# Expert operands as scaled fp16 pairs, and the last 64 slots of each expert in both column halves

## The chip, the cores and the metric

The kernel runs on one core of a Trainium2 chip. The metric is device time in microseconds for one execution; a program is timed in several runs, and their median counts. The engines are named as in the profile: PE is TensorE (matmuls), PEld its weight loads, DVE VectorE, ACT ScalarE, POOL GpSimd, SP SyncE, which here issues most of the DMA transfers. GpSimd issues the indirect ones (gathers and scatters by a list of row numbers).

## The reference, cut to what matters

An attention with a recurrent state (4 batches, 8 heads, 768 steps, head size 40) gives 3072 rows of 320 features. These rows go through a mixture of 8 experts, of which each row takes two:

```python
logits = x @ w_gate
noisy_logits = logits + np.log1p(np.exp(x @ w_noise)) * noise
top2 = np.argpartition(-noisy_logits, 2, axis=1)[:, :2]
...
for e in range(E):                       # E = 8
    for k in range(2):
        mask = top2[:, k] == e
        h = np.maximum(x[mask] @ w1[e], 0.0)          # 320 -> 1024
        out[mask] += top2_w[mask, k, None] * (h @ w2[e])   # 1024 -> 320
```

All inputs and the output are fp32.

## The kernel before, in words

**Stages.** The attention runs first, in 24 chunked steps. Each finished block of 128 rows is written to DRAM (`xd`) and gets its expert logits; after some blocks at a time `route` ranks the rows within their expert, and GpSimd scatters an entry for each row (row number, weight) into a list of slots per expert in DRAM (`ls`). `flag` then computes a word `fi`, which says whether the fast path was allowed. After that come the experts. At the end of the program every engine loads `fi` and branches: if it is set, a second pass with slots that overflowed (`extra`) runs, and behind it a general version of the whole.

**An expert** has 832 slots, in two parts of 512 and 320 (`PARTS`), or six tiles of 128 slots and one of 64. For each expert:

- SP loads the weights (`load1` into `w1r`, `load2` into `w2r`) and the slot list (`loadx` into `le`, which has two buffers; `w1r`, `w2r` and `xr` have one). GpSimd gathers the 832 rows into `xr`, one indirect transfer for each tile.
- `split1`, `split2`: each weight becomes a pair, its rounding (`w1h`, `w2h`, written by ScalarE) and the rest (`w1l`, `w2l`, written by VectorE).
- `trans`: TensorE transposes the rows into `pt`, and ScalarE and VectorE write them as pairs (`xh`, `xl`, and `x3`, `x3l` for the last 64 features).
- `hidden`: for each of 8 groups of 128 hidden features, 8 matmuls into one `ph` buffer (of three): high times high, low times high and high times low. ScalarE writes the relu as `hh`, VectorE the rest as `hl`.
- `output`: for each tile of slots, 24 matmuls of 320 columns into one `po` buffer (of three), ScalarE scales by the routing weight into `y`, and GpSimd adds `y` to the output rows by an indirect transfer that accumulates.

Both operands of these matmuls are `fp32r` tiles before. Of the tile with 64 slots the loaded operand is 64 columns wide: half of the array's columns stand unused.

**Order.** The code writes expert e's `hidden` and `output` with the loads, splits and transposes of expert e + 1 between them. The order on each engine is set by the tile framework's scheduler (`schedule_with_timeline_sim=True`), which simulates the program with its own costs. Each engine, and each queue of transfers that it issues, then works through its list in that order and waits where a semaphore says so. The first expert's part 0 has a priority, so that it starts while the last routing round runs. Its second part and all later experts read the list after the last scatter.

Of the kernel before, what the change touches and what calls it, by code (L numbers as in the profile page):

```python
# [41 lines left out]
class Moe:  # L42
# [180 lines left out]
    def split2(s,w):
        nc=s.nc
        h=s.wp.tile([128,8,DM],F32R,name="w2h"); l=s.wp.tile([128,8,DM],F32R,name="w2l")
        for k in range(0,8,2):
            nc.scalar.activation(h[:,k:k+2],w[:,k:k+2],AF.Copy)
            nc.vector.tensor_tensor(l[:,k:k+2],w[:,k:k+2],h[:,k:k+2].bitcast(F32),op=ALU.subtract)
        return h,l
    def loadx(s,e,X=None,part=0):  # L230
# [12 lines left out]
        return X
    def trans(s,x,X=None,part=0):

        nc=s.nc
# [4 lines left out]
        t0,n=s.parts[part]; t0%=CAP
        for k in range(3):
# [4 lines left out]
            if k<2:  # L257
                nc.scalar.activation(xh[:,k,r],pt[:,:n],AF.Copy)  # L258
                nc.vector.tensor_tensor(xl[:,k,r],pt[:,:n],xh[:,k,r].bitcast(F32),op=ALU.subtract)
            else:  # L260
                for q in (slice(0,64),slice(64,128)): nc.scalar.activation(x3[q,r],pt[64:128,:n],AF.Copy)
                for q in (slice(0,64),slice(64,128)): nc.vector.tensor_tensor(x3l[q,r],pt[64:128,:n],x3[64:128,r].bitcast(F32),op=ALU.subtract)
        return X
    def hidden(s,W,X,part):
        nc=s.nc; wh,wl=W; xh,xl,x3,x3l=X
        t0,n=s.parts[part]; t0%=CAP; r=slice(t0,t0+n)
        hh=s.hp.tile([128,8,n],F32R,name=f"hh{part}"); hl=s.hp.tile([128,8,n],F32R,name=f"hl{part}")
        for f in range(8):
# [605 lines left out]
```

## Time and profile before

| what | us |
|---|---|
| median of 3 runs | 1047.81 |
| the runs | 1039.84, 1050.55, 1047.81 |
| span of the profiled execution | 1041.6 |
| TensorE busy in it | 786.2 |
| VectorE, ScalarE, GpSimd busy | 498.1, 396.3, 473.4 |
| experts, about | 606 to 1030 |

The span is the time from the first to the last instruction that the profiler saw on the core. The profiled execution has no time of its own beside its span; the median of the runs stands 6.2 us above it. Times in the rows below count from the start of the span.

### The profile page before, as it was taken

What the parts mean: (1) busy time and instruction counts of PE and PEld (TensorE: products, weight loads), DVE (VectorE), ACT (ScalarE), POOL (GpSimd) and SP (SyncE); (2) the same over time, 40 slices, a digit from 0 to 9 for tenths busy, and PEclk for the clock granted to TensorE, in tenths of its full rate; (3) what the DMA queues carried; (4) which work ended last, traced back from release to release, by engine and by line L of the source; (5) the groups of instructions that cost most, each with busy time, mean ns of one, the idle gap of its engine ahead of it and who ended that gap; (6) DMA issues with size and microseconds to landing.
All of it is one profiled execution on the core that took longest, in us unless ns stands there. A gap on an engine that the chain in (4) does not pass through costs nothing.

```text
span 1041.6 us, 25165 instructions
## 1 busy us (share of the span) xinstructions
PE 786.2 (75%) x10570; PEld 696.0 (67%) x10570; DVE 498.1 (48%) x951; ACT 396.3 (38%) x816; POOL 473.4 (45%) x616
## 2 busy tenths in 40 slices
PE   0111043968767687998869469999999999999995
PEld 0111043757656575887658349999999999999995
DVE  9369924464566454456345442534343334433420
ACT  2213322444443353564434322534343434343421
POOL 6202478056786848818830324133333333333313
PEclk9999996789897886999969579999999999999998
DMA  3789863487488558665335743425252525252303
GB/s 100 184 199 254 237 175 79 114 220 203 121 205 235 101 128 216 161 149 146 89 82 157 228 151 62 132 49 136 59 135 60 140 56 137 57 139 57 36 7 38
DMA packets 135263, 136.20 MB, mean 131 GB/s; under 512 B 67392, under 2 KB 114948, under 8 KB 135060
## 3 DMA queue, kind: packets, MB, share of 16 engines
q1 hardware_dynamic: 123492, 117.35, 42.9%
q0 software_dynamic: 11648, 17.15, 9.3%
q8 instruction: 85, 1.39, 0.6%
q14 instruction: 38, 0.31, 0.1%
HBM read 96.48 MB, written 41.37 MB: 132 GB/s over the span
## 4 chain that ended last, share of the span: by engine, by line
PE 48%; POOL 18%; DMA 15%; DVE 7%; issue 5%; SPq 4%; ACT 2%; POOLq 0%; ACTq 0%; DVEq 0%
PE po L286 19%; PE ph L273 17%; POOL X L534 6%; POOL Tt L533 5%; POOL ls L161 3%; DMA rawk<-in_fm_dram 3%; PE pt L255 2%; DMA d_ab<-pk 2%; PE pY L433 2%; PE pW L433 2%; PE psc L433 2%; DMA xr<-xd,le 2%; DMA le<-ls 1%; DMA raww<-in_fm_dram 1%; DVE pk L423 1%
## 5 line engine op out<-in xcount | busy, mean ns | idle before, releaser
L289 POOL DMA_INDIRECT out_dram<-y,le x56 | 93.6, 1672 | 204.4 <-ACT y L288 202.3
L275 DVE SCALAR_TENSOR_TENSOR hl<-ph,hh 128x320 fp32r<-128x320 f32 (+1 forms) x128 | 75.4, 591 | 156.9 <-ACT hh L274 156.7
L274 ACT ACTIVATE hh<-ph 128x320 fp32r<-128x320 f32 (+1 forms) x128 | 66.1, 518 | 153.5 <-PE ph L273 153.4
L242 POOL DMA_INDIRECT xr<-xd,le x56 | 54.0, 964 | 92.0 <-DMA le<-ls 44.6
L534 POOL TENSOR_TENSOR X<-X,Tt 128x30 f32<-128x30 f32 (+9 forms) x150 | 85.2, 568 | 10.5
L286 PE MATMUL po<-w2h,hh 128*128 128x320 f32 (+1 forms) x448 | 87.2, 314 | 0.0
L533 POOL TENSOR_TENSOR Tt<-X 128x30 f32<-128x30 f32 (+9 forms) x150 | 81.6, 544 | 10.0
L286 PE MATMUL po<-w2l,hh 128*128 128x320 f32 (+1 forms) x448 | 78.2, 312 | 0.0
L286 PE MATMUL po<-w2h,hl 128*128 128x320 f32 (+1 forms) x448 | 77.6, 309 | 0.0
L286 PEld LDWEIGHTS po<-w2h,hh 128*128 128x128 f32 (+1 forms) x448 | 70.7, 180 | 4.2
L273 PE MATMUL ph<-xh,w1h 128*128 128x512 f32 (+1 forms) x256 | 71.3, 362 | 0.5 <-ACT xh L258 0.5
L273 PE MATMUL ph<-xh,w1l 128*128 128x512 f32 (+1 forms) x256 | 69.4, 352 | 0.0
L273 PE MATMUL ph<-xl,w1h 128*128 128x512 f32 (+1 forms) x256 | 69.0, 351 | 0.0
L433 PE MATMUL pQ<-w,dT 128*128 128x40 f16 x1152 | 41.6, 186 | 35.3 <-DMA d_k<-pk 27.2
L286 PEld LDWEIGHTS po<-w2h,hl 128*128 128x128 f32 (+1 forms) x448 | 67.6, 180 | 0.8
L286 PEld LDWEIGHTS po<-w2l,hh 128*128 128x128 f32 (+1 forms) x448 | 67.2, 180 | 1.2
L433 PEld LDWEIGHTS <-dT 128*128 128x128 f16 x1152 | 39.0, 101 | 42.8 <-DMA d_k<-pk 27.5
L433 PEld LDWEIGHTS <-st_ab 120*64 120x64 f16 (+1 forms) x928 | 26.6, 117 | 60.6 <-issue 26.6
L433 PE MATMUL psc<-RV,uT 128*64 128x128 f32 x384 | 59.8, 306 | 7.3 <-DVE P L657 6.8
L433 PE MATMUL psc<-RV 128*64 128x128 f32 x384 | 59.9, 306 | 0.0
L288 ACT ACTIVATE y<-po,le 128x320 f32<-128x320 f32 (+1 forms) x56 | 29.5, 526 | 79.1 <-PE po L286 79.1
L657 DVE TENSOR_TENSOR P<-psc,mk 128x512 f32<-128x512 f32 x48 | 33.0, 687 | 54.7 <-PE psc L433 54.6
(282 smaller groups left out, 1857.3 us busy)
## 6 DMA issues: line engine op xcount, KB each, us to landing
w2r<-in_w_dram SPq DMA_DIRECT2D x8, 1280.0 KB
RV<-in_rv_dram SPq DMA_DIRECT2D x48, 192.0 KB
rawba<-in_fm_dram SPq DMA_DIRECT2D x24, 360.0 KB
d_ab<-pk SPq DMA_DIRECT2D x24, 360.0 KB
st_ab<-d_ab SPq DMA_DIRECT2D x36, 240.0 KB
w1r<-in_w_dram SPq DMA_DIRECT2D x8, 1024.0 KB
raww<-in_fm_dram SPq DMA_DIRECT2D x12, 365.6 KB
st_ab<-d_ab SPq DMA_DIRECT2D x24, 180.0 KB
```

The lines of the kernel that those rows point to most:

```text
L161: st=nc.gpsimd.indirect_dma_start(out=s.ls[s.half],out_offset=OFFS(ap=po[:,j,k:k+1],axis=0),in_=s.ent[:,j,k],in_offset=None)
L242: for k in range(c,c+a): nc.gpsimd.indirect_dma_start(out=x[:p,k],out_offset=None,in_=s.xd[w],in_offset=OFFS(ap=li[:p,k,0:1],axis=0))
L273: for i,(a,b) in enumerate(mm): nc.tensor.matmul(ph[:,:n],a,b,start=i==0,stop=i==7)
L274: nc.scalar.activation(hh[:,f],ph[:,:n],AF.Relu)
L275: nc.vector.scalar_tensor_tensor(hl[:,f],ph[:,:n],0.0,hh[:,f].bitcast(F32),op0=ALU.max,op1=ALU.subtract)
L286: nc.tensor.matmul(po[:p],h[:,f,r],w[:,f],start=k==0,stop=k==23); k+=1
L288: nc.scalar.activation(y[:p],po[:p],AF.Copy,scale=w_[:p,ii:ii+1])
L289: st=nc.gpsimd.indirect_dma_start(out=s.out_d,out_offset=OFFS(ap=idx[:p,ii],axis=0),in_=y[:p],in_offset=None,compute_op=ALU.add)
L433: def mm(s,*a,**k): return lambda: s.nc.tensor.matmul(*a,**k)
L533: eng.tensor_tensor(t,Xt[:,j:j+1,j+1:].to_broadcast([128,j,m]),Xt[:,0:j,j:j+1].to_broadcast([128,j,m]),op=ALU.mult)
L534: s.tl=eng.tensor_tensor(Xt[:,0:j,j+1:],Xt[:,0:j,j+1:],t,op=ALU.add)
L657: nc.vector.tensor_tensor(m,pp.rearrange("p i j t->p (i j) t"),s.mk.to_broadcast([128,8,64]),op=ALU.mult)
```

## The change

The tiles of the expert operands become `F16`. So that high and low part lie in the range of fp16, the operands are scaled while they are split: rows by `XE` = 2^8, `w1` by `WE` = 2^6, `w2` by `VE` = 2^6; ScalarE's copy takes the scale, and VectorE's subtraction becomes one fused multiply and subtract. The routing weights take the inverse, `YS`, in `route`.

fp16 has less range, so guards are added, each a VectorE reduction into a column of its own. `sized` takes the maximum of a piece of each weight (256 or 320 elements in each partition) and of a tile of rows, which is compared with `LEAST` at the end. `finite` adds up `w1l` (2048 elements), the lower half of `w1h` (1024) and each `y` (320, or 160 in the last tile), and the sum is tested for being a number. `verdict` puts all of them together after the last expert, in nine VectorE instructions and one matmul, and writes `fi`. So `fi`, which was ready ahead of the experts, is ready only behind them.

In `output` the tile of 64 slots (c = 2) now has 48 matmuls of 160 columns: the 64 slots stand in the lower column half of the array with the first 160 output features and in the upper half with the others. Its `y` has 128 rows of 160 features, and the scatter writes half rows by the index `ix2` = 2 × row + half. For this the slot list of that tile is loaded into both halves of the partitions, with a fourth load of `le`.

```diff
+XE,WE,VE=2.0**8,2.0**6,2.0**6
+YS=1/(XE*WE*VE)
+LEAST=2.0**-9
...
         oh=s.gate(lg,s.nz[:,n0:n0+T],T,w[:,:,0],w[:,:,1])
+        nc.vector.tensor_scalar(w,w,YS,None,op0=ALU.mult)
...
+    def sized(s,a):
+
+        if s.nm<2*E_+1: s.nc.vector.tensor_reduce(s.mx[:,s.nm:s.nm+1],a,axis=AX.X,op=ALU.max); s.nm+=1
+    def finite(s,a,q=0):
+
+        s.nc.vector.tensor_reduce(s.yc[q:128,s.ny:s.ny+1],a,axis=AX.X,op=ALU.add); s.ny+=1
...
     def split1(s,w):
         nc=s.nc
-        h=s.wp.tile([128,3,FF],F32R,name="w1h"); l=s.wp.tile([128,2,FF],F32R,name="w1l")
+        h=s.wp.tile([128,3,FF],F16,name="w1h"); l=s.wp.tile([128,2,FF],F16,name="w1l")
         for k in (0,1,2):
-            nc.scalar.activation(h[:,k],w[:,k],AF.Copy)
-            if k<2: nc.vector.tensor_tensor(l[:,k],w[:,k],h[:,k].bitcast(F32),op=ALU.subtract)
-            else: nc.vector.tensor_tensor(h[64:128,k],w[64:128,k],h[64:128,k].bitcast(F32),op=ALU.subtract)
+            nc.scalar.activation(h[:,k],w[:,k],AF.Copy,scale=WE)
+            if k<2: nc.vector.scalar_tensor_tensor(l[:,k],w[:,k],WE,h[:,k],op0=ALU.mult,op1=ALU.subtract)
+            else: nc.vector.scalar_tensor_tensor(h[64:128,k],w[64:128,k],WE,h[64:128,k],op0=ALU.mult,op1=ALU.subtract)
+        s.sized(w[:,0,0:256])
+        s.finite(l.rearrange("p k f->p (k f)")); s.finite(h[64:128,2],64)
         return h,l
     def split2(s,w):
         nc=s.nc
-        h=s.wp.tile([128,8,DM],F32R,name="w2h"); l=s.wp.tile([128,8,DM],F32R,name="w2l")
+        h=s.wp.tile([128,8,DM],F16,name="w2h"); l=s.wp.tile([128,8,DM],F16,name="w2l")
         for k in range(0,8,2):
-            nc.scalar.activation(h[:,k:k+2],w[:,k:k+2],AF.Copy)
-            nc.vector.tensor_tensor(l[:,k:k+2],w[:,k:k+2],h[:,k:k+2].bitcast(F32),op=ALU.subtract)
+            nc.scalar.activation(h[:,k:k+2],w[:,k:k+2],AF.Copy,scale=VE)
+            nc.vector.scalar_tensor_tensor(l[:,k:k+2],w[:,k:k+2],VE,h[:,k:k+2],op0=ALU.mult,op1=ALU.subtract)
+        s.sized(w[:,0])
...
             nc.sync.dma_start(l[:p,c:c+a],s.ls[w][b:b+a*p].rearrange("(p a) f->p a f",p=p))
+            if p==64: nc.sync.dma_start(l[64:128,c:c+a],s.ls[w][b:b+a*p].rearrange("(p a) f->p a f",p=p))
...
-                nc.scalar.activation(xh[:,k,r],pt[:,:n],AF.Copy)
-                nc.vector.tensor_tensor(xl[:,k,r],pt[:,:n],xh[:,k,r].bitcast(F32),op=ALU.subtract)
+                nc.scalar.activation(xh[:,k,r],pt[:,:n],AF.Copy,scale=XE)
+                nc.vector.scalar_tensor_tensor(xl[:,k,r],pt[:,:n],XE,xh[:,k,r],op0=ALU.mult,op1=ALU.subtract)
...
-        hh=s.hp.tile([128,8,n],F32R,name=f"hh{part}"); hl=s.hp.tile([128,8,n],F32R,name=f"hl{part}")
+        hh=s.hp.tile([128,8,n],F16,name=f"hh{part}"); hl=s.hp.tile([128,8,n],F16,name=f"hl{part}")
...
+            c=128//p; d=DM//c
             k=0
             for h,w in ((hh,wh),(hl,wh),(hh,wl)):
                 for f in range(8):
-                    nc.tensor.matmul(po[:p],h[:,f,r],w[:,f],start=k==0,stop=k==23); k+=1
+                    for j in range(c): nc.tensor.matmul(po[p*j:p*j+p,:d],h[:,f,r],w[:,f,d*j:d*j+d],start=k==0,stop=k==23)
+                    k+=1
             y=s.yp.tile([128,DM],F32,name="y",bufs=8)
-            nc.scalar.activation(y[:p],po[:p],AF.Copy,scale=w_[:p,ii:ii+1])
-            st=nc.gpsimd.indirect_dma_start(out=s.out_d,out_offset=OFFS(ap=idx[:p,ii],axis=0),in_=y[:p],in_offset=None,compute_op=ALU.add)
+            nc.scalar.activation(y[:,:d],po[:,:d],AF.Copy,scale=w_[:,ii:ii+1])
+            s.finite(y[:,:d])
+            if c==1: o_,ix,yv=s.out_d,idx[:,ii],y
+            else:
+                ix=s.yp.tile([128,1],I32,name="ix2"); nc.vector.scalar_tensor_tensor(ix,idx[:,ii],2.0,s.half2,op0=ALU.mult,op1=ALU.add)
+                o_=s.out_d.rearrange("n (j d)->(n j) d",j=2); yv=y[:,:d]
+            st=nc.gpsimd.indirect_dma_start(out=o_,out_offset=OFFS(ap=ix,axis=0),in_=yv,in_offset=None,compute_op=ALU.add)
...
+        s.ny=s.nm=0
+        s.yc=t("yc",[128,E_*(NTT+5)]); nc.gpsimd.memset(s.yc,0.0)
+        s.mx=t("mx",[128,2*E_+1])
+        s.half2=t("half2",[128,1]); nc.gpsimd.memset(s.half2,0.0); nc.gpsimd.memset(s.half2[64:128],1.0)
+    def verdict(s):
+
+        nc=s.nc; t=lambda n,sh,dt=F32: s.kp.tile(sh,dt,name=n)
+        z=t("vz",[128,E_*(NTT+5)]); nc.vector.tensor_tensor(z,s.yc,s.yc,op=ALU.subtract)
+        nc.vector.tensor_scalar(z,z,0.0,None,op0=ALU.is_equal)
+        v=t("vv",[128,2*E_+2]); nc.vector.tensor_reduce(v[:,0:1],z,axis=AX.X,op=ALU.min)
+        nc.vector.tensor_scalar(v[:,1:],s.mx,LEAST,None,op0=ALU.is_ge)
+        vh=t("vh",[128,2*E_+2],F16); nc.vector.tensor_copy(vh,v)
+        pv=s.pt.tile([128,2*E_+2],F32,name="pt",bufs=2); nc.tensor.matmul(pv,s.ones,vh,start=True,stop=True)
+        b=t("vb",[128,2*E_+2])
+        nc.vector.tensor_scalar(b,pv,0.5,None,op0=ALU.is_lt)
+        nc.vector.tensor_scalar(b[:,0:1],pv[:,0:1],127.5,None,op0=ALU.is_lt)
+        w=t("vw",[128,1]); nc.vector.tensor_reduce(w,b,axis=AX.X,op=ALU.max)
+        g=t("vg",[128,2]); nc.vector.tensor_tensor(g,s.ff,w.to_broadcast([128,2]),op=ALU.max)
+        nc.vector.tensor_copy(s.fl,g)
...
             x=s.loadx(0); W1=s.split1(r1); X=s.trans(x[0])
+            s.sized(x[0][:,0])
...
             if e+1<E_: W2=s.split2(r2); x=xn
+        s.verdict()
```

`x3`, `x3l`, `hl` and the other tiles change in the same way.

**Order on SyncE**, in the middle of the experts: the issues of the loads for one expert (`w1r`, `w2r` weights, `le` slot list) and the first for the one after. Before:

```order
L208 DMA w1r<-in_w_dram 128x2x1024
L209 DMA w1r<-in_w_dram 64x1024 x2
L213 DMA w2r<-in_w_dram 128x8x320
L241 DMA le<-ls_843 128x16
L241 DMA le<-ls_843 128x8
L241 DMA le<-ls_843 64x4
L208 DMA w1r<-in_w_dram 128x2x1024
```

Now:

```order
L218 DMA w1r<-in_w_dram 128x2x1024
L219 DMA w1r<-in_w_dram 64x1024 x2
L254 DMA le<-ls_843 128x16
L254 DMA le<-ls_843 128x8
L254 DMA le<-ls_843 64x4
L255 DMA le<-ls_843 64x4
L223 DMA w2r<-in_w_dram 128x8x320
L218 DMA w1r<-in_w_dram 128x2x1024
```

The load of `w2r` stands behind the slot list instead of ahead of it. In the new program the first `le` of an expert waits for the scatter of tile 5 of the expert before, and no longer for its last one, which reads `ix2`.

**Order on TensorE**, in the first part of an expert's `hidden`: the place of the first transpose (`pt<-idm,xr`) of the next expert's rows. Before:

```order
L286 MATMUL po<-w2h,hh_12098 128x320 x3
L273 MATMUL ph<-xh,w1h 128x512 x2
L273 MATMUL ph<-x_11829,w1h 128x512
L273 MATMUL ph<-xh,w1l 128x512 x2
L273 MATMUL ph<-xl,w1h 128x512 x2
L273 MATMUL ph<-x3l,w1h 128x512
L286 MATMUL po<-w2h,hh_12098 128x320 x2
L255 MATMUL pt<-idm,xr 128x128 x2
L286 MATMUL po<-w2h,hh_12098 128x320
```

Now, where the weight load of each fp16 matmul is a row of its own:

```order
L287 LDWEIGHTS w1h
L287 MATMUL ph<-xl,w1h 128x512
L287 LDWEIGHTS w1h
L287 MATMUL ph<-x3l,w1h 128x512
L269 MATMUL pt<-idm,xr 128x128 x2
L301 LDWEIGHTS hh_10852
L301 MATMUL po<-w2h,hh_10852 128x320
L301 LDWEIGHTS hh_10852
```

Before, 56 matmuls of 512 columns and 14 of 320 of that expert stand ahead of the transposes; now 40 and 6. The next transposes follow behind 16 more matmuls of 512 and 6 of 320, in a group of four that reads the fourth tile too. The 48 matmuls of 160 columns stand in one block just ahead of each expert's first matmul, other than in the first expert, where some ten groups of them stand between other matmuls.

**Order on VectorE**, at the handover from the attention to the first expert: the splits of the first weights and the start of the last routing round (`xT`, `zc`). Before:

```order
L220 TENSOR_TENSOR w1l<-w1r,w1h 128x1024
L221 TENSOR_TENSOR w1h<-w1r,w1h 64x1024
L668 TENSOR_TENSOR xt<-pY,xt 128x320
L228 TENSOR_TENSOR w2l<-w2r,w2h 128x640 x4
L109 SCALAR_TENSOR_TENSOR xT<-px,xT 128x384
L171 TENSOR_SCALAR zc<-lg 128x16
```

Now:

```order
L230 SCALAR_TENSOR_TENSOR w1l<-w1r,w1h 128x1024
L231 SCALAR_TENSOR_TENSOR w1h<-w1r,w1h 64x1024
L215 TENSOR_REDUCE yc<-w1l 128x1
L212 TENSOR_REDUCE mx<-w2r 128x1
L215 TENSOR_REDUCE yc<-w1h 64x1
L711 TENSOR_TENSOR xt<-pY,xt 128x320
L240 SCALAR_TENSOR_TENSOR w2l<-w2r,w2h 128x640 x4
L212 TENSOR_REDUCE mx<-w1r 128x1
L212 TENSOR_REDUCE mx<-xr 128x1
L112 SCALAR_TENSOR_TENSOR xT<-px,xT 128x384
L273 SCALAR_TENSOR_TENSOR xl<-pt,xh 128x512 x2
L175 TENSOR_SCALAR zc<-lg 128x16
```

The guards (L212, L215) and the split of the first rows (`xl`) stand ahead of the last routing round. Part 1 of the first expert has moved on TensorE too: behind all 96 matmuls of `output` of its part 0, where it stood among them.

## Rows read from the trace of the kernel before

**Rows 1.** Chain that ended last: start us, length us, what.

```profile
773.01 5.50 PE ph L273 x24
...
824.83 5.50 PE ph L273 x24
...
981.31 5.51 PE ph L273 x24
```

**Rows 2.** Windows: busy us of PE, PEld, DVE, ACT, POOL; PEclk, DMA share, GB/s.

```profile
773.00:825.00 52.00, 52.00 (x320) 48.23 (x319) 20.72 (x32) 21.23 (x40) 18.57 (x14) 1.00 0.41 98
```

**Rows 3.** Timeline of PE at the end: start us, length us, what.

```profile
1025.15 1.33 PE L286 MATMUL po<-w2l,hh 128*128 128x320 f32 x8
1026.32 1.34 PE L286 MATMUL po<-w2h,hh 128*64 128x320 f32 x8
1027.49 1.33 PE L286 MATMUL po<-w2h,hl 128*64 128x320 f32 x8
```

**Rows 4.** Timeline of PE in the attention, fp16 matmuls.

```profile
456.04 0.45 PE L562 MATMUL pQ<-dm,idh 128*128 128x320 f16 x2
456.32 0.77 PE L433 MATMUL pQ<-w,dT 128*128 128x40 f16 x24
456.94 0.46 PE L433 MATMUL pst<-sfs,sel 128*120 128x320 f16 x2
...
461.96 0.43 PE L433 MATMUL pS<-sfs,ids 128*128 128x320 f16 x2
462.32 1.13 PE L433 MATMUL pY<-kb,P 128*64 128x40 f32 x32
463.28 0.43 PE L433 MATMUL psc<-st_ab,st_k 120*64 120x64 f16 x16
463.54 0.79 PE L433 MATMUL pS<-vu,kb 128*40 128x40 f32 x32
```

**Rows 5.** Lines by form, DVE, 570 to 1042: busy us, mean ns; idle before.

```profile
L303 DVE TENSOR_REDUCE ok<-fz 128x1 f32<-128x8 f32 x2 | 0.3, 152 | 0.0
L299 DVE TENSOR_REDUCE ok<-fz 128x1 f32<-128x128 f32 x1 | 0.3, 286 | 0.0
```

**Rows 6.** Windows in the first expert, columns as in rows 2.

```profile
616.00:620.00 4.00, 1.80 (x10) 1.29 (x11) 1.83 (x4) 1.36 (x4) 0.92 (x1) 1.00 0.21 61
620.00:623.60 3.60, 3.60 (x12) 2.93 (x11) 0.72 (x2) 0.12 (x1) 0.00 (x0) 0.53 0.02 7
```

**Rows 7.** Timeline of all engines around an expert's start: DMA issues.

```profile
822.19 1.55 POOL L289 DMA_INDIRECT out_dram<-y,le  x1 [2.01 <-ACT y L288]
...
827.98 0.39 SPq L213 DMA_DIRECT2D w2r<-in_w_dram  x1
...
832.32 1.32 SPq L241 DMA_DIRECT2D le<-ls  x3
...
836.67 1.01 POOL L242 DMA_INDIRECT xr<-xd,le  x1 [8.15 <-DMA le<-ls]
```

**Rows 8.** Tile y (scatter), 800 to 860, then tile le, 800 to 900: landing.

```profile
DMA to landing us min/median/max: 4.1/7.8/9.4
...
DMA to landing us min/median/max: 2.9/3.5/9.4
```

**Rows 9.** Tile xr, 800 to 900: landing of its gathers.

```profile
DMA to landing us min/median/max: 2.9/2.9/2.9
```

**Rows 10.** DMA, 820 to 840: GB/s in 40 slices of 0.5 us.

```profile
GB/s 0 41 77 184 26 0 0 0 41 49 169 69 0 0 0 0 0 0 77 79 307 374 261 335 397 397 392 221 2 3 0 0 0 0 0 0 82 225 21 154
```

**Rows 11.** Timeline at the handover, SP and POOL: DMA issues.

```profile
599.83 1.29 SPq L213 DMA_DIRECT2D w2r<-in_w_dram  x1
...
604.41 1.00 POOL L161 DMA_INDIRECT ls<-ent,po  x1 [1.51 <-DVE okh L308]
```

**Rows 12.** Tile ls, 590 to 640: landing of its scatters.

```profile
DMA to landing us min/median/max: 3.1/4.2/5.3
```

**Rows 13.** Line 851 at the end: ns min/median/max, first and last start us.

```profile
L851 PEldq COMPARE_BRANCH  x1: 3592/3592/3592, 1027.8 to 1027.8; - x1
```

More of the change, by code (lines that the diff above doesn't have):

```diff
@@ L247, in trans @@
         if X is None:
-            X=[s.xp.tile([128,2,s.cap],F32R,name="xh"),s.xp.tile([128,2,s.cap],F32R,name="xl"),
-               s.xp.tile([128,s.cap],F32R,name="x3"),s.xp.tile([128,s.cap],F32R,name="x3l")]
+            X=[s.xp.tile([128,2,s.cap],F16,name="xh"),s.xp.tile([128,2,s.cap],F16,name="xl"),
+               s.xp.tile([128,s.cap],F16,name="x3"),s.xp.tile([128,s.cap],F16,name="x3l")]
         xh,xl,x3,x3l=X
@@ L257, in trans @@
             if k<2:
-                nc.scalar.activation(xh[:,k,r],pt[:,:n],AF.Copy)
-                nc.vector.tensor_tensor(xl[:,k,r],pt[:,:n],xh[:,k,r].bitcast(F32),op=ALU.subtract)
-            else:
-                for q in (slice(0,64),slice(64,128)): nc.scalar.activation(x3[q,r],pt[64:128,:n],AF.Copy)
-                for q in (slice(0,64),slice(64,128)): nc.vector.tensor_tensor(x3l[q,r],pt[64:128,:n],x3[64:128,r].bitcast(F32),op=ALU.subtract)
+                nc.scalar.activation(xh[:,k,r],pt[:,:n],AF.Copy,scale=XE)
+                nc.vector.scalar_tensor_tensor(xl[:,k,r],pt[:,:n],XE,xh[:,k,r],op0=ALU.mult,op1=ALU.subtract)
+            else:
+                for q in (slice(0,64),slice(64,128)): nc.scalar.activation(x3[q,r],pt[64:128,:n],AF.Copy,scale=XE)
+                for q in (slice(0,64),slice(64,128)): nc.vector.scalar_tensor_tensor(x3l[q,r],pt[64:128,:n],XE,x3[64:128,r],op0=ALU.mult,op1=ALU.subtract)
         return X
@@ L274, in hidden @@
             nc.scalar.activation(hh[:,f],ph[:,:n],AF.Relu)
-            nc.vector.scalar_tensor_tensor(hl[:,f],ph[:,:n],0.0,hh[:,f].bitcast(F32),op0=ALU.max,op1=ALU.subtract)
+            nc.vector.scalar_tensor_tensor(hl[:,f],ph[:,:n],0.0,hh[:,f],op0=ALU.max,op1=ALU.subtract)
         return hh,hl
@@ L312, in flag @@
         nc.vector.tensor_scalar(c[:,2:3],pf[:,2:3],0.5,None,op0=ALU.is_lt)
-        f=t("ff",[128,2]); nc.vector.tensor_reduce(f[:,0:1],c[:,0:4],axis=AX.X,op=ALU.max); nc.vector.tensor_reduce(f[:,1:2],c,axis=AX.X,op=ALU.max)
-        s.fl=t("fi",[128,2],I32); nc.vector.tensor_copy(s.fl,f)
+        f=s.ff=t("ff",[128,2]); nc.vector.tensor_reduce(f[:,0:1],c[:,0:4],axis=AX.X,op=ALU.max); nc.vector.tensor_reduce(f[:,1:2],c,axis=AX.X,op=ALU.max)
+        s.fl=t("fi",[128,2],I32)
+        s.ny=s.nm=0
[16 more added lines that the diff above has]
+        nc.vector.tensor_copy(s.fl,g)
     def experts(s,after):
@@ L335, in extra @@
             s.output(s.split2(r2),s.hidden(s.split1(r1),s.trans(x[0]),0),x,e,0)
+        s.verdict()
 NP,NG,CG,C=2,6,2,64
```

## The prediction, before the run

> **What bounds the kernel now.** I read the chain that ended last first, because it tells which engine the end hangs on in each stage [rows 1]. The kernel has an attention stage and then eight experts, and in the experts the chain is a row of TensorE pieces: each expert begins with 24 matmuls of L273, at 773.01, 824.83 and 981.31. So one expert takes 824.83 − 773.01 = 51.8 us. Then I asked the table of stretches whether TensorE rests there [rows 2]: from 773 to 825 it is busy for 52.00 us of 52.00, at granted clock 1.00 (2.4 GHz), while VectorE has 20.7, ScalarE 21.2, GpSimd 18.6 and the DMA engines 0.41 of the stretch. There the time is the number of matmuls times their pace, and nothing else decides. The attention stage is left alone by the change, except for its last microseconds, into which the first expert's loads and splits are woven.
>
> **Matmul pace, in fp32r now.** A matmul's duration overlaps its neighbours, so I take distances between starts [rows 3]. Eight matmuls of 320 columns start at 1025.15 and the next eight at 1026.32: 1.17 us, or 147 ns each. The tile with 64 slots has the same pace (1026.32 to 1027.49). So a tile of 64 rows costs as much as one of 128, 24 × 0.147 = 3.5 us. For 512 columns, 24 take 5.50 us [rows 1], or 229 ns.
>
> **Matmul pace, in fp16.** The attention stage has fp16 matmuls of these shapes [rows 4]: two of 320 columns start at 456.04 and the next group at 456.32, 0.28 for two, some 135 to 140 ns; I take 135. Scaled by columns, 512 take 0.135 × 512/320 = 0.215 us. An expert has 64 matmuls of 512 columns (eight groups of eight), and 64 + 6 × 24 = 208 of 320 columns on full tiles. Gain: 64 × 14 ns = 0.9 and 208 × 12 ns = 2.5, together 3.4 us per expert. If the pace were as now, nothing; the fp16 rows could also be read as 140, then 208 × 7 and 64 × 5 leave 1.8.
>
> **The last tile.** It goes from 24 matmuls of 320 columns to 24 pairs of 160 columns, one in each column half of the array. Whether a pair overlaps is the question, and one row shows it: 16 fp16 matmuls of 64 columns, from two stores into two halves of `psc`, start at 463.28 and what follows starts at 463.54 [rows 4]. That is 0.26 us, 16 ns for each of 64 columns, which alone would stream for 64 × 135/320 = 27 ns. So pairs do run side by side, each with its own weight load. I take 160/320 × 135 = 68, rounded to 70 ns a pair: 24 × 70 = 1.7 us. The array changes its tiling twice in each expert: two fp16 matmuls of 320 took 0.36 us ahead of such a change (461.96 to 462.32) against 0.28 without it, so 0.08 to 0.1 each, 0.2 in all. New: 1.9; gain: 3.5 − 1.9 = 1.6 us. Bounds: without overlap 48 × 70 ns + 0.2 = 3.6, no gain; with a free change 1.8.
>
> So TensorE's work per expert falls by 3.4 + 1.6 = **5.0 us**, from 51.8 to about 46.8 (bounds: 1.7 and 5.5). Experts 1 to 7 give −35.0.
>
> The Trainium skill speaks against part of this: "TensorEngine Tiling (Array Packing)", sections Key Properties and Restrictions, says that column tiling switches off the fast weight load and that a change of the tiling mode drains the engine. By it the 48 loads of the small tile might set its pace. The row of 64-column pairs has two loads in 32 ns, so here the row disagrees with a large price; no run here shows 48 in a row behind full tiles.
>
> **VectorE's guards.** Two reductions give a slope [rows 5]: 128 elements take 286 ns, 8 take 152, so about 1.1 ns per element over 0.14. Per expert: 2048 elements 2.3 us, 1024 elements 1.3, 256 and 320 about 0.45, six tiles of y at 0.5 and one of 160 at 0.3: some 8 us. VectorE goes from 20.7 to 29 us of 47, so it doesn't become the bound. They lie beside TensorE's work; with three `ph` buffers a late `hl` stops it only after two groups more (3.4 us for 512 columns). ScalarE's copies with a scale and the fused subtractions have the shapes of the old ones; I cost them at nothing.
>
> **First expert.** At the handover the order puts five guards ahead of the last routing round: two of 256 to 320 elements, one of 2048, one of 1024 and one of the gathered rows, 5.4 us by the slope. They delay that round's scatter and so part 1 of the first expert. Now TensorE waits there: from 616 to 620 it is busy for 1.80 of 4.00, and then it runs at granted clock 0.53 for 3.6 us [rows 6], in which 1.7 us are lost: 3.9 together. In the new order part 1 stands behind all output matmuls of part 0 (96 × 135 ns = 13 us later), so this wait should go. Sum: −5.0 (matmuls) + 5.4 − 3.9 + 1.0 (some ten visits to the column halves in place of one) = **−2.5** for the start of expert 1; ends −9 (guards hidden) and +1.5 (wait stays).
>
> **A new wait in each expert.** Call T' the first matmul of an expert's L287 block. In the old order the first transpose of the next rows `xr` stands behind 56 matmuls of 512 and 14 of 320 (T + 14.9 us); in the new one behind 40 and 6: 40 × 0.215 + 6 × 0.135 = T' + 9.4. What feeds it: the scatter of tile 5 was issued at 822.19, 2.6 us ahead of T = 824.83 [rows 7]; the last tile behind it shrinks by 1.6, so T' − 1.0. Its landing takes 4.1 us at best, 7.8 in the median [rows 8], so T' + 3.1. The loads of `le` wait for it. They land in 2.9 at best [rows 8], and GpSimd issues `xr` at about T' + 6.2 (before, 836.67 − 832.32 = 4.35 after `le`, with `w2r` just ahead). A gather alone lands in 2.9 [rows 9]: T' + 9.1, just in time. But `w2r`, which was issued 4.3 us ahead of `le` (827.98), now follows four `le` issues of 0.44 each: T' + 4.9. Its 1.3 MB (128 × 8 × 320 floats) kept the DMA engines at 220 to 400 GB/s from about 1 to 6 us after its issue [rows 10], so T' + 6 to 11, on top of the gather. What a gather or scatter costs behind a weight load: the first `ls` scatter, issued at 604.41 with `w2r` from 599.83 in flight [rows 11], took 5.3 where the quickest took 3.1 [rows 12]. I take 2.9 + 2.2 = 5.1 to 5.3: landing at T' + 11.5, a wait of 2.1 us. Bounds: 0 (the queues share) and 4 (it lands behind the whole of `w2r`, T' + 11 + 2.4). Later gathers take 1.01 us each to issue, and the group of transposes that needs all four tiles stands 2 × 8 × 0.215 + 6 × 0.135 = 4.3 us behind the first, so only the first costs. Experts 1 to 6 have it: 6 × 2.1 = **+12.6** (0 to 24).
>
> **The end.** `verdict` adds some nine small VectorE operations (0.15 to 0.29 each) and a round through TensorE behind the last tile, about 3.5 us, and only then can the engines read the flag. Now TensorE's queue has its branch of 3.59 us at 1027.8 [rows 13], under matmuls that end near 1029.8; now it must follow the verdict. The drain of the last scatter, which follows in any case, hides part. I take +1.5; ends 0 and +4.
>
> **Sum.** −35.0 − 2.5 + 12.6 + 1.5 = −23.4. The profiled span of 1041.6 becomes 1018.2. The median of the runs, 1047.8, stands 6.2 above that span and I keep the 6.2: **1024.4 us**. One per cent, 10.5 us, is about what the three runs scatter by (1039.8 to 1050.6), and about what a measurement can tell from no change.
>
> **Rivals.**
> - *The wait isn't there.* The gather finds its share of the DMA engines beside `w2r`, or `le` lands earlier: −12.6, so 1012. For: the quickest landings were unaffected. Against: the scatter at 604.41. Chance 0.25. The Trainium skill, "DMA: Bandwidth & Descriptors", section Queues, rings and completion order, says that each DMA engine takes turns between the queues that have work, packet by packet; this rival is that rule. By it a gather of eight times fewer bytes would at most double its transfer.
> - *fp16 has no better pace in these streams, or the pairs don't overlap.* The weight load of 128 columns could set the pace as the fp32r one may do now. Gain of the last tile alone, 8 × 1.6 = 13, less start and end, against a shorter T': the wait shrinks too, to about 1 us. −13 + 6 + 1.5 − 1: about 1041. Pairs alone failing: 1024 + 13 = 1037. For: the fp16 stream of 320 columns is only two long in the trace. Against: 24 matmuls of 40 columns, each with its own load, take 0.62 us (456.32 to 456.94), so a load costs 26 ns at most. Chance 0.13 together.
> - *Slower: the wait grows and takes the clock with it.* If tile 5's scatter lands in 7.8 instead of 4.1, `le`, `xr` and the first transpose slip by 3.7 more, to a wait of 5.8; VectorE's `sized` of `w2r`, which stands ahead of four `hl`, waits for `w2r` in the same time and stops `ph` next. After a gap of that size the granted clock was 0.53 for 3.6 us [rows 6], another 1.7. 7.5 × 6 = 45 in place of 12.6: 1057, and with the slowest landing of that row, 9.4, 1.6 × 6 more: 1066. It decides from a wait of about 6 us per expert. For: 7.8 is the median of these landings now. Against: the quick ones are those at an expert's end, where tile 5 is, with no weight load in flight. Chance 0.12, a part of it (waits of 4 to 5 us) near 1040.
> - *A guard trips or a flag goes up*, and the second pass over all experts runs, and behind it the general version of everything: hundreds of us more. The inputs are plain normal draws, far above the floor of 2^-9. Chance 0.01.
>
> My forecast has 0.49. **Range** 1006 to 1046: below, no wait and the guards at the handover hidden; above, the pairs or the pace failing, or waits of about 5 us. Faster by over 1% (below 1037.3): 0.49 + 0.25, less the upper tail of the forecast, which shades into waits of 4 us: 0.72. Within 1%: 0.20, from that tail, the second rival and the milder half of the third. Slower by over 1%: 0.08.
>
> **What would show it.** Distances between starts of 135 and 215 ns, and 70 ns a pair in one block of 48; TensorE busy about 47 of 49 us per expert, with one idle time of about 2 us ahead of the first transpose, ended by the DMA of `xr`; VectorE near 29 us per expert; clock 1.00 throughout; some 12 to 13 us from the last matmul to the end. I am wrong if the idle time is elsewhere (`hl` late, then VectorE or its wait for `w2r` is the bound), if the clock falls after it, or if the pairs take 140 ns.

## The result, and the profile after

The changed kernel takes 1031.3 us (median of 4 runs, 1026.6 to 1034.7) against 1044.4 of the kernel before (4 runs in all): ratio 0.986, 95% interval 0.982 to 0.991, or 13 us faster. The forecast was 23 us faster, 1024.4; the time lies in its range, 1006 to 1046. The profiled span is 1029.4 us.

First the chain of the profile after, as in [rows 1]; and the piece of the one before that tells where its expert 1 began.

```profile
668.02 5.48 PE ph L273 x24
```

```profile
666.96 4.64 PE ph L287 x21
...
723.77 5.30 PE ph L287 x24
...
775.01 5.30 PE ph L287 x24
...
823.02 5.30 PE ph L287 x24
828.71 6.71 DMA xr<-xd,le
...
874.36 5.30 PE ph L287 x24
...
973.19 5.29 PE ph L287 x24
```

Expert 1 starts 1.1 us earlier. Experts 1 to 6 take 973.19 − 666.96 = 306.2 us, where before they took 981.31 − 668.02 = 313.3. The last expert's matmuls end near 1017.0: 43.8 us, against 48.5. From there to the end it is 12.4 us, 11.8 before. So −1.1 − 7.1 − 4.7 + 0.6 = −12.3, nearly all of the difference of the spans. And a gather (`DMA xr`) now stands in the chain for 6.7 us.

The pace on TensorE at the end of the profile after, which answers to [rows 3]:

```profile
1013.02 1.25 PE L301 MATMUL po<-w2h,hl 128*128 128x320 f16 x8
1014.11 1.25 PE L301 MATMUL po<-w2l,hh 128*128 128x320 f16 x8
1015.29 0.74 PE L301 MATMUL po<-w2h,hh 128*64 128x160 f16 x16
1015.87 0.72 PE L301 MATMUL po<-w2h,hl 128*64 128x160 f16 x16
1016.42 0.72 PE L301 MATMUL po<-w2l,hh 128*64 128x160 f16 x16
```

Eight of 320 columns take 1.09 us, 136 ns each. Eight pairs of 160 take 0.55 to 0.58, 69 to 72 ns a pair. Between the tilings 1.18 stands in place of 1.09, a change of 0.09 us.

The windows of two experts, and of a piece of the second (columns as in [rows 2]):

```profile
775.01:823.02 48.01, 47.06 (x342) 30.54 (x343) 27.34 (x43) 20.64 (x39) 18.90 (x15) 1.00 0.43 106
823.02:874.36 51.34, 48.45 (x342) 31.08 (x343) 27.58 (x43) 20.64 (x39) 19.08 (x15) 0.97 0.40 99
832.00:835.40 3.40, 0.57 (x3) 0.08 (x1) 0.21 (x1) 0.60 (x1) 2.49 (x4) 0.93 1.06 381
835.40:839.50 4.10, 4.04 (x15) 2.08 (x16) 0.88 (x2) 0.04 (x1) 1.51 (x2) 0.64 0.35 114
```

TensorE is idle from about 832.6 to 835.4, while the DMA engines are full (1.06, 381 GB/s), and then runs for some 4 us at a granted clock of 0.64 on average, between its two levels (2.4 GHz and 1.2 GHz). What ended the wait, in the timeline of that stretch, which answers to [rows 7]:

```profile
826.15 1.33 SPq L254 DMA_DIRECT2D le<-ls  x3
827.53 0.59 SPq L255 DMA_DIRECT2D le<-ls  x1
828.23 0.53 SPq L223 DMA_DIRECT2D w2r<-in_w_dram  x1
828.71 1.01 POOL L256 DMA_INDIRECT xr<-xd,le  x1 [0.98 <-PE ph L287]
...
835.19 0.49 DVE L212 TENSOR_REDUCE mx<-w2r 128x1 f32<-128x320 f32 x1 [3.39 <-DMA w2r<-in_w_dram]
...
835.46 0.69 PE L269 MATMUL pt<-idm,xr 128*128 128x128 f32 x2 [2.89 <-DMA xr<-xd,le]
```

With T' = 823.02, `le` is issued at T' + 3.1 and `xr` at T' + 5.7, 0.5 us behind `w2r`. `w2r` has landed when VectorE's `mx` starts at 835.19, and 0.27 us later the gather is there too.

The queues tell what of the gather is late: q1 is SyncE's, which carries `w2r`, and q0 GpSimd's, which carries the gathers (packets, MB, share of the 16 engines). First from 829.4 to 833.4, then from 833.4 to 835.4:

```profile
q1 hardware_dynamic: 923, 1.17, 94.7%
xr<-xd,le POOLq DMA_INDIRECT x4, 4.2
```

```profile
q0 software_dynamic: 167, 0.60, 84.2%
q1 hardware_dynamic: 127, 0.14, 20.9%
```

In the first 4 us gathers are being issued (the second row), and their queue moves nothing; then 0.60 MB pass in 2 us. So the gather starts late, and its transfer is short.

In the expert before, the issue of `w2r` itself took 1.24 us, and the transposes waited for 0.95 us only:

```profile
780.55 1.24 SPq L223 DMA_DIRECT2D w2r<-in_w_dram  x1
780.92 1.01 POOL L256 DMA_INDIRECT xr<-xd,le  x1 [1.18 <-PE ph L287]
...
785.51 0.44 PE L269 MATMUL pt<-idm,xr 128*128 128x128 f32 x2 [0.95 <-DMA xr<-xd,le]
```

The early gathers go with a slow issue of `w2r`: it takes 1.24 us in expert 3 and 2.03 in expert 6 (930.95), whose transposes wait little or not at all, and 0.52 to 0.53 in the four others, which wait for 2.5 to 6.2 us. Why some issues are slow stays open.

### The profile page after: what moved, and what is told of

Same layout as the page of the kernel before. It is cut to its first block, busy times and chain, and to the rows that moved or that the text cites. A ratio compares the mean times of both kernels' runs of the same rounds, so it can differ in the third digit from the quotient of the medians.

```text
span 1029.4 us, 25672 instructions
## 1 busy us (share of the span) xinstructions
PE 758.2 (74%) x10763; PEld 559.8 (54%) x10763; DVE 556.8 (54%) x1062; ACT 393.9 (38%) x816; POOL 475.3 (46%) x619
## 4 chain that ended last, share of the span: by engine, by line
PE 43%; DMA 15%; POOL 15%; issue 12%; DVE 9%; ACT 3%; SPq 3%; POOLq 0%; ACTq 0%; DVEq 0%
PE po L301 13%; PE ph L287 13%; POOL X L577 4%; DMA xr<-xd,le 3%; POOL Tt L576 3%; POOL ls L165 3%; PE pY L476 3%; PE pW L476 3%; PE psc L476 2%; DMA rawk<-in_fm_dram 2%; PE pt L269 2%; DMA X<-scr 2%; POOL out_dram L310 1%; PE pQ L476 1%; DMA rawba<-in_fm_dram 1%
## 5 line engine op out<-in xcount | busy, mean ns | idle before, releaser
L289 DVE SCALAR_TENSOR_TENSOR hl<-ph,hh 128x320 f16<-128x320 f32 (+1 forms) x128 | 74.6, 589 | 104.0 <-ACT hh L288 103.8
L288 ACT ACTIVATE hh<-ph 128x320 f16<-128x320 f32 (+1 forms) x128 | 65.6, 517 | 162.2 <-PE ph L287 161.0
L287 PEld LDWEIGHTS <-w1h 128*128 128x128 f16 x768 | 75.6, 100 | 58.0 <-issue 7.5
L301 PEld LDWEIGHTS <-hh 128*128 128x128 f16 (+1 forms) x1024 | 83.9, 101 | 37.5 <-issue 4.0
L301 PE MATMUL po<-w2h,hh 128*128 128x320 f16 (+1 forms) x512 | 77.3, 287 | 0.9 <-ACT hh L288 0.9
L301 PE MATMUL po<-w2h,hl 128*128 128x320 f16 (+1 forms) x512 | 70.8, 283 | 0.0
L287 PE MATMUL ph<-xh,w1h 128*128 128x512 f16 (+1 forms) x256 | 68.6, 353 | 1.8 <-DVE hl L289 1.3
L301 PE MATMUL po<-w2l,hh 128*128 128x320 f16 (+1 forms) x512 | 69.6, 283 | 0.0
L287 PE MATMUL ph<-xh,w1l 128*128 128x512 f16 (+1 forms) x256 | 67.9, 347 | 0.0
L287 PE MATMUL ph<-xl,w1h 128*128 128x512 f16 (+1 forms) x256 | 66.7, 343 | 0.0
L165 POOL DMA_INDIRECT ls<-ent,po x48 | 50.4, 1050 | 24.6 <-DVE po L158 12.3
L476 PEld LDWEIGHTS psc<-RV,uT 128*64 128x64 f32 x384 | 47.8, 155 | 14.2 <-issue 6.4
```

What stands on the lines that cost most here:

```text
L165: st=nc.gpsimd.indirect_dma_start(out=s.ls[s.half],out_offset=OFFS(ap=po[:,j,k:k+1],axis=0),in_=s.ent[:,j,k],in_offset=None)
L287: for i,(a,b) in enumerate(mm): nc.tensor.matmul(ph[:,:n],a,b,start=i==0,stop=i==7)
L288: nc.scalar.activation(hh[:,f],ph[:,:n],AF.Relu)
L289: nc.vector.scalar_tensor_tensor(hl[:,f],ph[:,:n],0.0,hh[:,f],op0=ALU.max,op1=ALU.subtract)
L301: for j in range(c): nc.tensor.matmul(po[p*j:p*j+p,:d],h[:,f,r],w[:,f,d*j:d*j+d],start=k==0,stop=k==23)
L476: def mm(s,*a,**k): return lambda: s.nc.tensor.matmul(*a,**k)
```

## The experiments

The twelve runs fell on four chips. On two of them the kernel before takes 1040 and 1043 us, on the other two 1070. Ratios are each to the kernel before on the same chip; between chips I compare only the time of one expert, from its first L287 matmul to the next expert's.

**Runs 1 to 4 (before: 1040.1 us).**

A third buffer for the slot list:

```diff
-l=s.xp.tile([128,NTT,4],F32,name="le",bufs=2)
+l=s.xp.tile([128,NTT,4],F32,name="le",bufs=3)
```

> The changed kernel with a third buffer for the slot list le, and nothing else. The list and the gather of an expert's rows then no longer wait for the scatters of the expert ahead. My theory (the gather is late because le is freed late and w2r is issued ahead of it; the idle time and the clock after it cost about 20 us over experts 1 to 6): gaps ahead of the first transposes gone, 47.3 to 47.6 us per expert, total about 1010. Rival (VectorE with its guards, or the earlier place of the transposes, holds TensorE): the order still has the guards and the transposes early, so the gaps move but stay, 1025 to 1031.

1005.0 us, ratio 0.965 (0.958 to 0.972). The windows of two experts:

```profile
712.17:759.02 46.85, 46.85 (x345) 30.56 (x342) 27.50 (x43) 20.76 (x39) 18.80 (x15) 1.00 0.43 108
759.02:805.86 46.84, 46.84 (x343) 30.56 (x342) 27.50 (x43) 20.74 (x39) 18.78 (x15) 1.00 0.45 109
```

TensorE doesn't rest, the clock stays, and VectorE carries the same guards (27.5 us). So here the guards hold nothing up. Experts 2 to 6, without a wait, take 46.84 us each. Expert 1 is longer here too:

```profile
661.78:712.17 50.39, 48.34 (x348) 31.07 (x348) 32.51 (x53) 21.93 (x42) 21.79 (x18) 1.00 0.50 132
```

It holds six more transposes than the others (27 and 21), and rests of 1.2 and 0.85 us. The six together take 284.6 us: of the changed kernel's 306.2 the third buffer takes away 21.6 us, waits and what the clock took behind them. (The two traces are of two chips of the same kind.)

Without the guards:

```diff
-        s.nc.vector.tensor_reduce(s.yc[q:128,s.ny:s.ny+1],a,axis=AX.X,op=ALU.add); s.ny+=1
+        pass
...
-        s.verdict()
```

(`sized` is emptied in the same way, and `fi` is written in `flag` again.)

> The changed kernel without its guards: no sized, no finite, no verdict; the flag is written where it was before. The order around the first transposes (40 and 6 matmuls ahead, le ahead of w2r) is as in the changed kernel. My theory: the gaps of about 3 us and the half clock after them stay in experts 2, 4, 5; only the handover (up to 5 us) and the end (0.5) gain: 1024 to 1029. Rival (VectorE's guards hold TensorE): the gaps go, 1010 to 1013.

1024.2 us, ratio 0.983 (0.976 to 0.990). The wait is where it was:

```profile
814.54:866.17 51.63, 48.80 (x345) 30.97 (x342) 20.70 (x32) 20.63 (x39) 19.10 (x15) 0.97 0.40 98
```

```profile
827.00 0.44 PE L269 MATMUL pt<-idm,xr 128*128 128x128 f32 x2 [2.83 <-DMA xr<-xd,le]
```

51.6 us with 20.7 of VectorE, as 51.3 with 27.6: for experts 2 to 6 the rival falls. Expert 1 is another matter. It takes 51.1 us where the changed kernel has 56.8, and waits 2.3 us for its rows and not 6.2:

```profile
664.47:715.59 51.12, 48.80 (x344) 30.92 (x342) 21.99 (x35) 20.65 (x40) 18.70 (x15) 0.97 0.44 110
```

So part of what expert 1 loses goes with the guards. Its slot list is issued 3.9 us behind the expert's start here, 6.0 in the changed kernel; by what step the guards delay it was not tried.

The last tile as before, in fp16 and with its guard:

```diff
-                    for j in range(c): nc.tensor.matmul(po[p*j:p*j+p,:d],h[:,f,r],w[:,f,d*j:d*j+d],start=k==0,stop=k==23)
+                    nc.tensor.matmul(po[:p],h[:,f,r],w[:,f],start=k==0,stop=k==23)
...
-            if p==64: nc.sync.dma_start(l[64:128,c:c+a],...)
```

> The changed kernel with the last tile as before: 24 matmuls of 320 columns into 64 rows, no second load of le, no half-row scatter. The scheduler then returns to the old order: w2r ahead of le, first transposes behind 56 and 14 matmuls. My theory (the half-column tile frees le earlier and so brings the new order and the wait): last tile +1.6 us in each of 8 experts, +13, and about 15 of the 20 us of waits go: 1026 to 1031, about the same as the changed kernel. Rival (the wait is not tied to the half-column tile): gaps of 3 us stay and the time is 1042 to 1046.

1017.7 us, ratio 0.979 (0.972 to 0.986), better than I had expected. The changed kernel had 0.986 (0.982 to 0.991) on its chip; by the ratios this is some 7 us better, but the intervals overlap. The edit takes out the pairs, the fourth load of `le` and the half-row scatter together. `w2r` stands ahead of `le` again and the first transposes behind 56 and 14 matmuls. Experts take 48.5 and 49.8 in turn:

```profile
758.97:807.49 48.52, 48.52 (x319) 31.38 (x318) 27.65 (x42) 20.87 (x39) 18.50 (x14) 1.00 0.43 105
807.49:857.31 49.82, 48.85 (x318) 31.28 (x318) 27.65 (x42) 20.86 (x39) 18.50 (x14) 1.00 0.41 102
```

Both edits:

> Both: third buffer for le, and the last tile as before. Against the kernel with the third buffer alone this is the price of the half-column tile with no gather in the way: by my sum 8 x 1.6 = 13 us slower than that one, about 1023. If pairs in the two column halves do not overlap, the two are alike.

1014.9 us, ratio 0.975 (0.968 to 0.983). Experts 2 to 6 take 48.44 us each, with no rest:

```profile
761.15:809.59 48.44, 48.44 (x318) 31.38 (x318) 27.57 (x42) 20.86 (x39) 18.85 (x15) 1.00 0.42 104
```

Against 46.84 the half-column tile is worth 1.60 us per expert. The medians of runs 1 and 4 differ by 9.9 us where 8 × 1.6 = 13 was expected, with about 10 us between the slowest and the quickest run of run 4's kernel. So the same edit that saves some 10 to 13 us brought the order in which about 22 are lost.

**Runs 5 to 8 (before: 1070.2 us).**

Half of each `w2` (the rest is split from the first half again):

```diff
-        nc.sync.dma_start(w,s.w2_d[e].rearrange("(k p) d->p k d",p=128))
+        nc.sync.dma_start(w[:,:4],s.w2_d[e].rearrange("(k p) d->p k d",p=128)[:,:4])
```

> The changed kernel, but only the first half of each w2 is loaded (0.66 MB in place of 1.31) and split twice, so that its second half of hidden features uses the weights of the first; the rest of the work and its order are as in the changed kernel. My theory (the gather lands only when the w2r load that was issued just ahead of it has passed): landing of the first gather about 2.5 us earlier, gaps of experts 2, 4, 5 from 3 us to 0 to 1, clock stays at 1.00 behind them, expert 1 some 3 us shorter: 1016 to 1021. Rival (the gather is slow by itself, by scatters or by the list): gaps stay, 1028 to 1031.

1045.6 us, ratio 0.977 (0.973 to 0.980); the time itself says little, since this chip's attention stage is slower (the first matmul of the experts stands at 622 us, at 608 in the profile after). The experts answer the question: 47.8 to 48.3 us each in experts 2 to 6, the clock at 1.00, where the unedited kernel has 51.2 to 53.2 on a chip of this kind (run 9):

```profile
740.08:788.23 48.15, 47.07 (x345) 30.53 (x342) 27.47 (x43) 20.76 (x39) 19.23 (x15) 1.00 0.40 92
```

```profile
793.88 1.01 POOL L256 DMA_INDIRECT xr<-xd,le  x1 [0.57 <-PE ph L287]
...
798.78 0.44 PE L269 MATMUL pt<-idm,xr 128*128 128x128 f32 x2 [0.93 <-DMA xr<-xd,le]
```

That gather was used 4.9 us after its issue, where 6.75 passed in the changed kernel, and the rests of experts 2 to 6 are 0.8 to 1.3 us, against 2.6 to 3.4 in run 9. In these experts the wait follows the size of the load ahead. Expert 1 does so only in part: it takes 55.3 us and still waits 4.7, 1.5 us shorter than in the changed kernel where I had expected 3.

`w2r` behind the fourth gather:

```diff
+        if e and s.cap==CAP: s.tc.add_manual_dep(d.ins,s.g3.ins.name,mybir.DependencyInfo(mybir.DependencyClass.Sync,mybir.DependencyReason.DATA),reason="after")
```

(`d` is the load of `w2r`, `g3` the gather of tile 3.)

> The changed kernel, but the load of w2r waits until the fourth gather of the next expert's rows has landed. Order on TensorE the same up to the first transpose (40 and 6 matmuls ahead). My theory: the first gather lands in about 2.9 us, T' + 9.1, so no gap over 0.5 us in experts 2 to 6 and no fall of the clock: 1011 to 1018. Rival (the chain of scatter, list and gather is too long without w2r as well): gaps of 1.5 us and more remain, 1022 to 1028.

1060.0 us, ratio 0.990 (0.987 to 0.993). Half of the expectation came true. In the timeline of an expert with T' = 797.28:

```profile
802.99 1.01 POOL L258 DMA_INDIRECT xr<-xd,le  x1 [0.63 <-PE ph L290]
...
806.74 0.38 PE L272 MATMUL pt<-idm,xr 128*128 128x128 f32 x2
...
809.76 0.39 SPq L223 DMA_DIRECT2D w2r<-in_w_dram  x1
...
817.00 0.49 DVE L212 TENSOR_REDUCE mx<-w2r 128x1 f32<-128x320 f32 x1 [6.39 <-DMA w2r<-in_w_dram]
...
818.14 0.69 PE L290 MATMUL ph<-xh,w1h 128*128 128x320 f16 x2 [2.47 <-DVE hl L292]
```

In experts 2 to 6 the gather's wait is gone: the transposes run at T' + 9.5 and wait for nothing. (Expert 1 still waits 3.0 us for its gather and takes 54.9.) But `mx<-w2r`, the guard, waits 6.4 us for the later load, three `hl` stand behind it, and TensorE waits 2.5 us for those. An expert still takes 50 to 52 us. That is the second clause of the prediction's slow rival (`sized` ahead of `hl`), reached by another way: here a guard does hold TensorE up, through what it waits for.

The third buffer in the kernel before (same line as in run 1):

> The kernel before with a third buffer for le. Before, only three gaps of 0.3 to 1.0 us in all stood ahead of transposes, so my theory gives 1 to 4 us: 1036 to 1040, where the kernel before has 1040 on this chip. Rival (the gain of the third buffer has nothing to do with the new order): about 20 us, 1020.

1078.4 us, ratio 1.008 (1.004 to 1.012): a loss of 0.8%. The order puts the first transposes behind 24 matmuls there too, and TensorE waits 1.0 us for `hl` in each of experts 2 to 6, 53.2 us. So the buffer brought no gain to this kernel. But on this kind of chip it brings none to the changed kernel either (run 10), so the run doesn't tell whether the kernel or the chip is the reason.

No guards, with the third buffer (the edits of runs 1 and 2):

> Third buffer for le, and no guards (no sized, no finite, no verdict). Where no gather is waited for, my sum has the guards cost only the end (0.5) and something at the handover (up to 5): 1000 to 1005, against 1005 with them. Rival (29 us of VectorE work per expert hold TensorE up): more than 0.5 us in each expert, 996 to 1000.

1074.4 us, ratio 1.005 (1.002 to 1.007), with 53 to 56 us in experts 2 to 5 (50.9 in 6) and many rests of 0.3 to 1.1 us between matmuls which the profile ends with "issue". Neither theory had that, so it tells nothing of the guards. It raised another question: whether run 1 would do the same on this kind of chip.

**Runs 9 to 11 (before: 1070.3 us).**

The changed kernel, unedited:

> The changed kernel once more, for a comparison with the third buffer on one chip. My theory: gaps of about 3 us ahead of the first transposes in experts 2, 4 and 5, 51.3 us each, none or a small one in experts 3 and 6, as in its first profile; 0.98 to 0.99 of the kernel before.

1067.5 us, ratio 0.997 (0.994 to 1.000). The rests ahead of the transposes are 2.6 to 3.4 us in experts 2 to 6, in 3 and 6 too, and an expert takes 51.2 to 53.2. All six issues of `w2r` take 0.52 to 0.54 us here, so none lets a gather through early:

```profile
804.54:855.70 51.16, 48.52 (x345) 31.04 (x342) 27.35 (x43) 20.62 (x39) 19.02 (x15) 0.97 0.41 100
```

The kernel of run 1:

> The third buffer once more: 46.8 us per expert again, and 0.96 to 0.97 of the kernel before, whatever the attention stage takes on this chip; 18 to 25 us ahead of the changed kernel.

1071.0 us, ratio 1.000 (0.998 to 1.002): the expectation fails. Experts 2 to 6 take 54.4 to 54.6 us where they took 46.84.

```profile
794.96:849.55 54.59, 49.94 (x344) 30.69 (x342) 27.33 (x43) 20.62 (x38) 18.72 (x15) 0.97 0.40 93
```

```profile
799.12 0.39 PE L287 MATMUL ph<-xh,w1h 128*128 128x512 f16 x1 [0.20 <-issue]
...
800.56 0.38 PE L287 MATMUL ph<-xh,w1l 128*128 128x512 f16 x1 [0.35 <-issue]
...
801.96 0.38 PE L287 MATMUL ph<-x3l,w1h 128*128 128x512 f16 x1 [0.60 <-issue]
...
803.40 0.65 PE L269 MATMUL pt<-idm,xr 128*128 128x128 f32 x4 [0.44 <-issue]
```

No gather is waited for in experts 2 to 6. TensorE stops between matmuls that need nothing new, 4 to 9 us behind the expert's start, while the gathers run: 1.2 to 1.7 us in sum. Then it waits 2.59 us for a late `hl`, and that comes from the other side of TensorE:

```profile
794.14 0.89 PE L301 MATMUL po<-w2l,hh 128*64 128x160 f16 x16
...
803.44 0.39 ACT L304 ACTIVATE y<-po,le 128x160 f32<-128x160 f32 x1 [3.10 <-PE ph L287]
803.51 3.03 DVE L240 SCALAR_TENSOR_TENSOR w2l<-w2r,w2h 128x640 f16<-128x640 f32 x4 [9.30 <-PE ph L287]
...
807.55 1.01 PE L287 MATMUL ph<-xh,w1h 128*128 128x512 f16 x2 [2.59 <-DVE hl L289]
```

The last matmuls of the small tile stand at 794 to 795, but ScalarE's `y` and VectorE's `w2l`, which need them, wait for TensorE until 803.4, 8.5 us behind the expert's start. `hl` stands behind that `w2l`. In run 1 the same `y` comes 2.1 us behind its expert's start (759.02) and the same `w2l` 0.3:

```profile
761.10 0.37 ACT L304 ACTIVATE y<-po,le 128x160 f32<-128x160 f32 x1
```

So, by these rows, TensorE's finished matmuls reach the other engines late on this chip. What delays them stays open.

Guards over one column:

```diff
+        a=a[:,0:1]
```

(in `sized` and in `finite`, with the third buffer)

> Third buffer, and every guard reduces one column in place of its 160 to 2048, so that nearly the same instructions stand in nearly the same order and only VectorE's time for them goes (some 7 us per expert; the guards then see less of the data). My theory (VectorE has room in the experts): 46.8 us per expert as with whole guards, gain only at the handover, 0 to 4 us in all. Rival (the guards cost TensorE time): 46.3 or less per expert.

1079.6 us, ratio 1.009 (1.006 to 1.012), 54 to 56 us in experts 2 to 5 (49.5 in 6), with the rests of run 8. It can't speak of the guards either.

**Run 12 (before: 1042.8 us).** The kernel of run 3:

> The changed kernel with the last tile as before, once more, to see whether its gain (0.979 of the kernel before on the first chip) holds on another chip, where the third buffer's did not. My theory (the gain of the fp16 pace stands on TensorE alone, and in this order the gathers stay clear of the weight load and the small tile): 48.5 to 49.9 us per expert and 0.975 to 0.985 of the kernel before. Rival (fp16 streams are held up on that chip wherever gathers run): 51 us per expert and more, 0.99 to 1.01.

1018.8 us, ratio 0.977 (0.971 to 0.984), experts of 48.5 and 49.6 to 50.1 us in turn. It repeats run 3, but on a chip of the first kind, so how this version does on the second kind stays open.

## Why the prediction was right, and where it was off

- **Pace and last tile.** Right: 136 ns forecast as 135, 69 to 72 ns a pair forecast as 70, 0.09 us for a change of tiling. "From 51.8 to about 46.8" is the 46.84 of run 1. The split of the 5.0 came out less well: 3.4 us for the pace and 1.6 for the last tile were forecast, and by run 4 it is about 3.1 and 1.9 (an estimate: run 4 gains 3.4, in which its own last tile has some 24 × 11 ns). The 1.60 between runs 4 and 1 is not that 1.6: it counts from a tile that is in fp16 already, the forecast's from one in fp32r. So the sum to the tenth is in part luck, as is the 135, which was taken from rows that could also be read as 140. The Trainium skill's "TensorEngine Tiling (Array Packing)", section Restrictions, says that column tiling switches off the fast weight load. No price of that shows here: a pair of 160 columns, with its two loads, takes 69 to 72 ns, where 320 columns take 136.
- **The new wait.** Right in place, cause and sign, and too small in size: this is the term that was mis-sized. I put +12.6 (0 to 24) for experts 1 to 6; by run 1 it is 21.6. Three things are in that. The gather is used 6.75 us after its issue (T' + 12.4), and I had it landing 5.1 to 5.3 after (T' + 11.5): I took the middle, and it came as in the far bound, behind the whole of `w2r`, though 1 us earlier than that bound's T' + 13.4. The clock falls behind each of the rests of 2.5 us and more (in expert 4 to 0.64 over some 4 us); I had put that only into the slow rival, "from a wait of about 6 us", and had named it as a sign that I am wrong. Rests of 2.5 to 2.9 us and the clock together cost 4.4 to 4.5 in experts 2, 4 and 5, where 2.1 was forecast. And expert 1, which I counted like the others, lost 6.4 against its time in run 1: its list is issued 6.0 us behind its start, and its transposes rest for 6.2 us. Experts 3 and 6 lost 1.2 and 0.7.
- **The difference in one line.** Start, six experts, wait, last expert, end: forecast −2.5 − 30 + 12.6 − 5 + 1.5 = −23.4; found −1.1 − 28.7 + 21.6 − 4.7 + 0.6 = −12.3. The wait makes 9.0 of the 11.1 us.
- **The cause of the wait** is shown from three sides: less to load ahead (run 5) shortens it, loading behind (run 6) ends it in experts 2 to 6, and fetching the list early (run 1) ends it there too. That the half-column tile, with its list and scatter, brought the order is shown by run 3. The guards don't make the wait of experts 2 to 6 (run 2), but they have a part in that of expert 1.
- **The first rival** (queues share) didn't come true: the first gather begins to move only when `w2r` is almost through. By the Trainium skill, "DMA: Bandwidth & Descriptors", section Queues, rings and completion order, a DMA engine takes turns, packet by packet, between the queues that it has work for. These rows don't go against that: GpSimd's queue moved no packet for 4 us, and the trace doesn't say whether it had none ready or was not served. Only where the issue of `w2r` itself was slow (780.55 and 930.95) did the gather come through early.
- **VectorE's guards.** About 7 us per expert, 20.7 to 27.5 (forecast 8), and hidden in experts 2 to 6 of runs 1 and 2. They cost something at the two ends: nine of the verdict's ten VectorE operations run from 1017.96 to 1020.4, and the end grew by 0.6 us, forecast 1.5.
- **First expert.** −1.1 in place of −2.5. What was argued of its parts (guards at the handover, the wait for part 1) wasn't tried one by one.
- **Slips in the working.** The upper bound of the gain per expert is 3.4 + 1.8 = 5.2 and not 5.5; the five guards at the handover come to 5.1 by the slope and not 5.4, which makes the start −2.8; and [rows 10] show 220 to 400 GB/s from 2 to 6 us behind the issue of `w2r`, not from 1. No verdict hangs on them.
- **The other kind of chip.** There the gain is 0.3% and not 1.4%. Part of it is that every expert has the wait. Why TensorE's stream stops on "issue" there in the third-buffer kernels, and why its finished matmuls reach the other engines late, and neither on the first kind, stays open.

The version with a third buffer beats both kernels (1005 us) on the one chip of the first kind where it ran; on the one of the other kind it beats neither.

## What to carry to other kernels

A small gain on the bounding engine can move a buffer's release, and with it the order of transfers: look at what the freed load now stands beside, and count the wait at its far bound when a gather is issued just behind a large load. Add what the clock takes behind the rest: here it was some 1.6 to 1.9 us per expert behind rests of 2.5 to 2.9 us. And time a change of order on more than one chip, since waits that are hidden on one may not be on the next.

## What the hardware showed that was not expected

- A gather of 128 rows, issued 0.5 us behind a load of 1.3 MB, was used 6.75 us after its issue, at the end of that load; behind half of it, 4.9; where the load's own issue took 1.24 us, 4.6; with none ahead, at most 3.75 (run 6).
- Chips differ by 3% on the same program (the kernel before: 1040 and 1070 us). In the changed kernel's two profiles, 1029.4 and 1069.4 us, 29 of the 40 us lie ahead of expert 1. In one expert of run 1's kernel it is 16% (46.84 and 54.5 us).
- In that kernel `y` of the small tile follows 2.1 us behind the next expert's start on the one chip and 8.5 us behind it on the other, though the matmuls that it needs stand at nearly the same place in both.
